# VectorE's decay passes in a fixed order, piece by piece, with the constant tables behind the first piece

## The chip, the cores and the metric

One core of a Trainium2 chip runs the whole program. The metric is the device time of one execution in microseconds; several executions are timed and their median is given. One execution is also profiled. Engines are named as in the profile: PE (TensorE matmul), PEld (TensorE weight load), DVE (VectorE), ACT (ScalarE), POOL (GpSimd) and SP (SyncE, which here only issues transfers).

## The reference

Three layers follow each other. The first is causal attention with a learned decay, for 4 batches of 8 heads, 576 positions, head size 64:

```
s_pos = np.maximum(s, 0.0)
cum = np.cumsum(s_pos, axis=-1)
bias = -(cum[:, :, :, None] - cum[:, :, None, :])
scores = np.where(causal, -1000000000.0, scores + np.minimum(bias, 0.0))
```

followed by a softmax over the row and the product with `v`. The second is a gated layer, `(x @ w1) * (x @ w2) @ w3 @ w_out`, over 2304 tokens, and the third a soft mixture of 8 experts with 4 slots each. The change concerns `cum` alone, the running sum of the positive part of `s` for each of the 32 heads.

## The kernel before

**The decay rows.** `cum` of all 32 heads is made once, at the start, on 32 partitions (one head each). The scores of a head are one matmul over 68 rows: 64 rows of q or k, and 4 rows that hold `cum` in a high and a low part, with their negatives and with ones, so that the product adds `cum_k - cum_q` to the score. `decay_fetch` loads `s` into `dec`. `decay_rows` then works on DVE, with one pass on ACT for each piece:

- `steps(c0, c1)`: L150 takes the positive part times 8, L153 the running sum (the scan of the second stretch starts from the last column of the first).
- for each piece (columns 0 to 320, 320 to 512, 512 to 576): L169 rounds the sum to the matmul's type (high part), L170 subtracts that from the sum (low part), L171 on ACT negates the high part, L172 negates the low part.

`steps` runs twice, for columns 0 to 320 and 320 to 576. The tiles `rows_0` (high) and `rows_1` (low) hold columns up to 512, `rows_2` both parts of the rest. POOL fills the ones of these tiles at L163.

**Who reads them.** The first attention items need query tiles 0 to 2 alone, so columns 0 to 320. Items 0 and 1 (`n < NDIR`) take their rows straight from `rows_0` and `rows_1` by two transfers each (L322, high part first). All later items take them from the DRAM copy `rows_d`, which `decay_store` writes (L176 twice, L177) and L324 reads back.

**What sets the order.** SP's instructions run in program order: `s`, the first word block, q/k of item 0, the second word block, q/k of item 1, the four L322, q/k of item 2 (L300), a word block (L188), L176 twice, L177, q/k of item 3, L324 of item 2, and so on. The order on DVE, ACT, POOL and PE is written by a planner before the run: it lays the program out against its own timeline and places an instruction when what it needs is ready there, so an engine can take later work while an earlier chain waits. A dependency marked `NoSync` between two instructions of one engine fixes their order and adds no semaphore.

**The constant tables.** `masks` builds `rep`, `sel4` and `half` (L789, L791, L794), and `choice_rows`, written at the very end of the program, builds `part` (L962, L965). They need only `ident`, and the planner has put them among the decay passes. `rep`, `sel4`, `half` and `part` are read much later.

**The rest of the start.** Weights come as 64-bit words: `load_words` turns a block into floats with L202 (ACT), L205, L206, L209 (DVE), L233 (ACT) and L234 (POOL). The scores are L359 (PE), the row minimum L362 (DVE), the exponential L367 (ACT), the normalisation L376 and L377 (DVE) and L380 (POOL), the transposes L395 and L409 (PE).

Of the kernel before, what the change touches and what calls it, by code (L numbers as in the profile page):

```python
# [11 lines left out]
F32R = mybir.dt.float32r  # L12
# [4 lines left out]
ALU = mybir.AluOpType  # L17
AX = mybir.AxisListType
# [10 lines left out]
NS = NE * SPE  # L29
# [18 lines left out]
def attn_glu_softmoe_kernel(  # L48
# [14 lines left out]
    nc = tc.nc  # L63
# [55 lines left out]
    ident = cp.tile([P, P], F32, name="ident")  # L119
# [24 lines left out]
    def decay_rows():  # L144
        t0 = dec[0]
        ones = t0[:, 1]
        nc.gpsimd.memset(ones, 1.0)

        def steps(c0, c1):
            nc.vector.tensor_scalar(  # L150
                out=t0[:, 0, c0:c1], in0=t0[:, 0, c0:c1], scalar1=0.0, scalar2=8.0, op0=ALU.max, op1=ALU.mult
            )
            nc.vector.tensor_tensor_scan(  # L153
                out=t0[:, 2, c0:c1], data0=ones[:, c0:c1], data1=t0[:, 0, c0:c1],
                initial=t0[:, 2, c0 - 1 : c0] if c0 else 0.0, op0=ALU.mult, op1=ALU.add,
            )

        rows = [wp.tile([NH, 2, 2, 512], F32, tag="W", name=f"rows_{a}", bufs=NW) for a in range(2)]
        rest = gq.tile([NH, 2, 2, 2, S - 512], F32, tag="g4", name="rows_2", bufs=NG4)
        dec[:] = rows + [rest]  # L160
        for x in rows + [rest]:
            for n in range(2):
                nc.gpsimd.memset(x[:, n, n] if x is not rest else x[:, :, n, n], 1.0)  # L163
        for c0, c1 in ((0, 320), (320, 512), (512, S)):
            if c0 < 512:
                steps(c0, c1 if c1 < 512 else S)
            cum = t0[:, 2, c0:c1]
            p0, p1 = (x[:, :, :, c0:c1] for x in rows) if c1 <= 512 else (rest[:, 0], rest[:, 1])
            nc.vector.tensor_copy(p0[:, 0, 1].bitcast(F32R), cum)  # L169
            nc.vector.tensor_tensor(out=p1[:, 0, 1].bitcast(F32R), in0=cum, in1=p0[:, 0, 1], op=ALU.subtract)  # L170
            nc.scalar.activation(out=p0[:, 1, 0], in_=p0[:, 0, 1], func=AF.Copy, scale=-1.0)  # L171
            nc.vector.tensor_scalar(out=p1[:, 1, 0], in0=p1[:, 0, 1], scalar1=-1.0, scalar2=None, op0=ALU.mult)  # L172

    def decay_store():
        for a in range(2):
# [106 lines left out]
    hd = {}  # L282
# [470 lines left out]
    def run(steps):  # L753
        for _, f in steps:
            f()

    with tc.tile_pool(name="att", bufs=1) as ap:
        phi_sb = ap.tile([P, KC, NS], F32, name="phi_sb")
        u_sb = ap.tile([P, FC, NS], F32, name="u_sb")
        decay_fetch()  # L760
        fetch_words(0, ap)
        att_fetch(0, ap)
        fetch_words(1, ap)
        att_fetch(1, ap)
        make_identity(nc, ident)
        mask = ap.tile([P, S], F32, name="mask")
        nc.gpsimd.memset(mask, 0.0)
        nc.gpsimd.affine_select(
            out=mask[:, S - P :], in_=mask[:, S - P :], pattern=[[-1, P]], base=0,
            channel_multiplier=1, compare_op=ALU.is_ge, fill=NEG,  # L770
        )
        hd["mask"] = mask
        hd["ap"] = ap
        att = att_steps(ap)
        decay_rows()
        for n in range(NDIR):
            att_prep(n, ap)
        att_fetch(2, ap)
        for k in range(2, NRAW):
            fetch_words(k, ap)  # L780
        decay_store()
        for n in range(NDIR, FAR):
            att_fetch(n + 1, ap)
            att_prep(n, ap)

        def masks():

            rep = cp.tile([P, NS], F32, name="rep")
            nc.vector.tensor_reduce(out=rep, in_=ident.rearrange("p (r s) -> p s r", s=NS), axis=AX.X, op=ALU.add)  # L789
            sel4 = cp.tile([P, 4, NS], F32, name="sel4")  # L790
            nc.vector.tensor_copy(sel4, rep.unsqueeze(1).broadcast_to([P, 4, NS]))  # L791

            half = cp.tile([P, 1], F32, name="half")
            nc.vector.tensor_reduce(out=half, in_=ident[:, :64], axis=AX.X, op=ALU.add)  # L794
            return rep, sel4, half

        def load(k):
            i = k // 2 - 1
            if FC <= i < N0:
                (sum_rows if k % 2 else use_rows)(*TODO[i])  # L800
            if k < 2 * N0:
                load_words(k, ap)
            if k + NRAW < 2 * N0:
                fetch_words(k + NRAW, ap)

        def fetch_later(i):
            if i > N0:
                store_words(i - 1)
            if i < len(TODO):
                for e in range(2):  # L810
                    fetch_words(2 * i + e, ap)

        prep = [(1, lambda k=k: load(k)) for k in range(2 * N0 + 2)]
        more = []
        for i in range(N0, len(TODO)):
            more += [(1, lambda i=i: fetch_later(i)), (1, lambda: None)]
            more += [(1, lambda k=2 * i + e: load_words(k, ap)) for e in range(2)] + [(1, lambda: None)]
        more.append((1, lambda: fetch_later(len(TODO))))
        run(weave(att[0], prep[:CA]))
        rep, sel4, half = masks()  # L820
        nc.sync.dma_start(phi_sb, phi)
        steps, late = glu_steps(0, [])
        n1 = int(len(att[1]) * A1)
        run(weave(weave(att[1][:n1], steps[:GB1]), prep[CA:CB1]))
        run(weave(weave(att[1][n1:], steps[GB1:GB]), prep[CB1:CB]))
        k = GC - GB
        steps = steps[GB:]
        run(weave(att[2], weave(steps[:k], prep[CB:]) + steps[k:]))
        for b in range(2, B):
            steps, late = glu_steps(b - 1, late)  # L830
            n = len(more) // (B - b)
            run(weave(weave(att[b + 1], steps), more[:n]))
            more = more[n:]
# [68 lines left out]
    for a in range(0, 4, 2):  # L902
        zt_ps = psum("tp", f"zt_ps_{a}")
        for c in range(2):
            nc.tensor.transpose(zt_ps[:, c * P : (c + 1) * P], z_acc[:, (a + c) * P : (a + c + 1) * P], ident)
        nc.vector.tensor_reduce(
            out=zt[:, a : a + 2], in_=zt_ps[:, : 2 * P].rearrange("p (c t s) -> p c s t", t=2, s=2 * NS),
            axis=AX.X, op=ALU.add,
# [49 lines left out]
    def choice_rows():  # L958
        cb = c_all.rearrange("p (b t) s -> p b t s", t=5)

        for k, m in enumerate((8, 16)):
            nc.vector.tensor_reduce(  # L962
                out=part[:, k, 0:1], in_=ident.rearrange("p (a r s) -> p a r s", r=2, s=m)[:, :, 1], axis=AX.XY, op=ALU.add
            )
        nc.vector.tensor_scalar(  # L965
            out=part[:, :, 1:2], in0=part[:, :, 0:1], scalar1=-2.0, scalar2=1.0, op0=ALU.mult, op1=ALU.add
        )
# [6 lines left out]
        for i4 in range(B):  # L974
# [7 lines left out]
            for blk, (t0, nt, tiles) in enumerate(BLK):  # L982
                tp = psum("sg", f"ctr_ps_{i4}_{blk}")
                for i in tiles:
                    q0, r = QT[i]
# [6 lines left out]
                    out=dst, in0=tp[:, :nt], scalar=part[:, 0, 0:1], in1=dst.bitcast(F32), op0=ALU.mult, op1=ALU.add  # L992
# [34 lines left out]
    order = mybir.DependencyInfo(mybir.DependencyClass.NoSync, mybir.DependencyReason.DATA)  # L1027
# [113 lines left out]
```

## Time and profile before

| | |
|---|---|
| median of 3 runs | 550.87 us (547.64 to 552.92) |
| the profiled execution | 552.43 us |
| its span in the trace | 550.7 us |
| granted TensorE clock, mean | 0.993 |
| busy: PE / DVE / ACT / POOL | 516.8 / 329.0 / 311.6 / 130.6 us |
| instructions | 11764 |

The span is the time from the first to the last instruction of the profiled execution; the 1.7 us between it and that execution's own time lie before and after it. Times in the rows below are microseconds from the start of the span. An engine's busy time leaves out its waits, and PE's ends are modelled.

### The profile page before, as it was taken

Reading aid. Unit: us, or ns where it says so; the run is one execution under the profiler, and the core shown is the slowest. Engines: PE = TensorE matmul, PEld = TensorE weight load, DVE = VectorE, ACT = ScalarE, POOL = GpSimd, SP = SyncE. Lnnn points to the kernel's source line nnn. Section 1 sums busy time; section 2 is a strip of 40 time slices with the busy share of each in tenths; the row PEclk is TensorE's granted clock in tenths of the full one; section 3 lists DMA queues with packets and bytes.
Section 4 is the critical chain, followed back from the end, with each engine's and each line's share of the span. In section 5 each row is a group of like instructions: output and inputs, shape, how many; then the busy total and the mean of one; then the engine's idle time right before and its main releaser. Section 6 shows DMA issues by size and latency. Waiting matters only on the chain.

```text
span 550.7 us, 11764 instructions
## 1 busy us (share of the span) xinstructions
PE 516.8 (94%) x4288; PEld 434.3 (79%) x4288; DVE 329.0 (60%) x1016; ACT 311.6 (57%) x845; POOL 130.6 (24%) x199
## 2 busy tenths in 40 slices
PE   2799899998999999999999999999999999989993
PEld 2567678877788898999989889899989999843452
DVE  7558787879987394866577668566630311252433
ACT  4567667687986674866577567558644211321222
POOL 4475563102454232110221311111310000000000
PEclk9999989999999999999999999999999999999998
DMA  5746973977673253563656537553514999689977
GB/s 147 235 146 193 280 223 128 292 259 269 218 253 102 73 161 113 169 201 133 194 170 211 173 99 208 176 172 114 167 44 137 413 411 376 241 293 423 420 295 241
DMA packets 38809, 118.03 MB, mean 214 GB/s; under 512 B 4224, under 2 KB 10560, under 8 KB 35296
## 3 DMA queue, kind: packets, MB, share of 16 engines
q1 hardware_dynamic: 36768, 113.60, 61.0%
q10 hardware_dynamic: 1984, 3.69, 2.4%
q8 instruction: 34, 0.56, 0.4%
q14 instruction: 23, 0.19, 0.1%
HBM read 102.11 MB, written 11.60 MB: 206 GB/s over the span
## 4 chain that ended last, share of the span: by engine, by line
PE 70%; DMA 13%; DVE 8%; ACT 4%; issue 2%; POOL 1%; SPq 0%; ACTq 0%; DVEq 0%; POOLq 0%
PE gl L457 31%; PE sc_ps L359 7%; PE x_ps L110 7%; PE pt_ps L395 5%; DMA raw_w<-in_w 5%; PE gn_ps L627 3%; PE o_ps L1042 3%; DMA raw_w3t<-in_w3t 3%; PE h_ps L1004 3%; PE ptd_ps L409 2%; PE z_ps L110 2%; DMA raw_wot<-in_wot 2%; DVE sc L362 1%; PE lg L110 1%; ACT sc L367 1%
## 5 line engine op out<-in xcount | busy, mean ns | idle before, releaser
L457 PE MATMUL gl<-x,w12t 128*128 128x320 f32 (+1 forms) x1536 | 237.7, 304 | 0.1
L457 PEld LDWEIGHTS gl<-x,w12t 128*128 128x128 f32 x1536 | 212.7, 190 | 7.4 <-issue 4.4
L380 POOL TENSOR_SCALAR sc<-sc,rinv 128x64 f32<-128x64 f32 (+4 forms) x160 | 101.1, 650 | 253.0 <-DVE rinv L377 85.7
L367 ACT ACTIVATE sc<-sc,nmax 128x64 f32<-128x64 f32 (+4 forms) x160 | 89.8, 563 | 31.4 <-DVE nmax L362 29.1
L362 DVE CUSTOM_DVE_ANT_0 sc<-sc_ps,mask 128x64 f32<-128x64 f32 (+4 forms) x160 | 65.0, 423 | 31.8 <-PE sc_ps L359 31.0
L397 ACT COPY pt<-pt_ps 128x128 f32<-128x128 f32 (+3 forms) x128 | 53.0, 426 | 34.1 <-PE pt_ps L395 25.1
L395 PE MATMUL pt_ps<-ident,sc 128*128 128x128 f32 x320 | 56.6, 286 | 5.5 <-POOL sc L380 3.2
L395 PEld LDWEIGHTS pt_ps<-ident,sc 128*128 128x128 f32 x320 | 38.4, 144 | 16.9 <-POOL sc L380 7.2
L463 ACT COPY a<-gl 128x256 f32<-128x256 f32 (+1 forms) x64 | 25.4, 398 | 46.0 <-PE gl L457 40.7
L359 PE MATMUL sc_ps<-qa 128*128 128x64 f32 (+1 forms) x144 | 46.4, 334 | 1.3 <-DVE gT L475 0.8
L110 PE MATMUL x_ps<-pt,v 128*64 128x256 f32 (+1 forms) x384 | 47.4, 358 | 0.0
L359 PE MATMUL sc_ps<-raw 68*128 68x288 f32 (+4 forms) x96 | 35.8, 516 | 11.6 <-DMA raw<-rows 9.8
L359 PE MATMUL sc_ps<-qb 68*128 68x64 f32 (+1 forms) x144 | 43.6, 306 | 0.9 <-DMA qb<-qa 0.9
L110 PEld LDWEIGHTS x_ps<-pt,v 128*64 128x64 f32 x384 | 33.5, 140 | 5.8 <-issue 1.0
L359 PEld LDWEIGHTS sc_ps<-raw 68*128 68x128 f32 x96 | 21.6, 265 | 16.9 <-issue 14.1
L202 ACT ACTIVATE w_w<-raw_w 128x512 f32<-128x512 f32 x32 | 21.6, 676 | 17.8 <-DMA raw_w<-in_w 17.7
L445 DVE TENSOR_TENSOR x<-x_ps,x 128x320 fp32r<-128x320 f32 (+1 forms) x32 | 14.1, 452 | 29.2 <-ACT x L444 29.2
L630 ACT COPY gn<-gn_ps 128x512 f32<-128x512 f32 x40 | 22.5, 584 | 15.5 <-PE gn_ps L627 15.1
L367 ACT ACTIVATION_READ_ACCUMULATOR sc<-sc,nmax 128x1 f32 x160 | 30.9, 193 | 0.0
L359 PEld LDWEIGHTS sc_ps<-qa 128*128 128x128 f32 x144 | 27.4, 190 | 3.6 <-DVE gT L475 1.3
L409 PE MATMUL ptd_ps<-ident,sc 128*128 128x128 f32 x160 | 25.9, 286 | 3.2 <-ACT pt L397 3.0
L359 PEld LDWEIGHTS sc_ps<-qb 68*128 68x128 f32 x144 | 27.4, 191 | 1.6 <-DVE v_sb L276 1.0
(180 smaller groups left out, 725.6 us busy)
## 6 DMA issues: line engine op xcount, KB each, us to landing
ew<-in_ew SPq DMA_DIRECT2D x27, 1024.0 KB
raw_w<-in_w SPq DMA_DIRECT2D x32, 512.0 KB
raw<-in_qk SPq DMA_DIRECT2D x24, 576.0 KB
v<-in_v SPq DMA_DIRECT2D x16, 576.0 KB
raw_w3t<-in_w3t SPq DMA_DIRECT2D x16, 512.0 KB
raw_wot<-in_wot SPq DMA_DIRECT2D x8, 512.0 KB
raw_wo<-in_wo SPq DMA_DIRECT2D x8, 512.0 KB
w_d<-w_w SPq DMA_DIRECT2D x8, 512.0 KB
```

The source lines that it names most:

```text
L110: mm = nc.tensor.matmul(out_, lhs, rhs, start=start, stop=stop)
L202: line_up(nc.scalar.activation(out=w, in_=hi.bitcast(F32), func=AF.Copy, scale=F64_SCALE))
L359: nc.tensor.matmul(pp[:r, : z - a], x[:, 0, q0 : q0 + r], x[:, 1, a:z], start=x is mul[0], stop=x is mul[-1])
L362: nc.vector.tensor_tensor_reduce(out=sc[:r, a:z], in0=pp[:r, : z - a], in1=hd["mask"][:r, m0 : m0 + z - a], scale=-0.125, scalar=3.0e38 if ...
L367: nc.scalar.activation(out=sc[:r, :W], in_=sc[:r, :W], func=AF.Exp, bias=nmax[:r, i : i + 1], scale=-1.0, accum_out=rsum[:r, i, 0:1],)
L380: nc.gpsimd.tensor_scalar(out=sc, in0=sc, scalar1=rinv[:, i : i + 1], scalar2=1.0, op0=ALU.mult, op1=ALU.mult)
L395: nc.tensor.transpose(tp[:, j * P : (j + 1) * P], sc[:, j * P : (j + 1) * P], ident)
L397: t["turned", i] = nc.scalar.copy(out=pt[:, p0 : p0 + step * (i - 1) + 1 : step], in_=tp[:, : i * P].rearrange("p (j q) -> p j q", q=P))
L409: nc.tensor.transpose(dg[:, p0 : p0 + P], t["sc"][:, c0 : c0 + P], ident)
L457: nc.tensor.matmul(acc[:, :nt], w12_t[fc][:, wi, n, kc], x_t[b, blk, kc][:, xi], start=k == 0, stop=k == 3 * KC - 1)
L463: st["a_copy"] = nc.scalar.copy(out=a_sb[:, :nt], in_=acc[:, :nt])
L630: st["turned", blk, k, h] = nc.scalar.copy(out=gn[:r, 4 * h : 4 * h + 4].rearrange("p c f -> p (c f)"), in_=tp[:r])
```

## The change

Every DVE pass of `decay_rows` is now passed through `line`, which makes it follow the previous one on DVE: L150, L153, L169, L170, L172 of columns 0 to 320, then L150 and L153 of columns 320 to 576, then L169, L170, L172 of columns 320 to 512, and the same three of 512 to 576. The last DVE pass of the first piece is kept as `hd["first"]`, and `after_first` makes four reductions for the tables (`rep`, `half` and the two of `part`) follow it; `sel4` and L965 follow these by their data. Line numbers of before. ACT's passes, the memsets, the transfers and the word conversions have no new dependency.

```diff
+        order = mybir.DependencyInfo(mybir.DependencyClass.NoSync, mybir.DependencyReason.DATA)
+        seq = []
+
+        def line(step):
+            for p in seq:
+                tc.add_manual_dep(step.ins, p.ins.name, order, reason="order")
+            seq[:] = [step]
+
         def steps(c0, c1):
-            nc.vector.tensor_scalar(
+            line(nc.vector.tensor_scalar(
                 out=t0[:, 0, c0:c1], in0=t0[:, 0, c0:c1], scalar1=0.0, scalar2=8.0, op0=ALU.max, op1=ALU.mult
-            )
-            nc.vector.tensor_tensor_scan(
+            ))
+            line(nc.vector.tensor_tensor_scan(
                 out=t0[:, 2, c0:c1], data0=ones[:, c0:c1], data1=t0[:, 0, c0:c1],
                 initial=t0[:, 2, c0 - 1 : c0] if c0 else 0.0, op0=ALU.mult, op1=ALU.add,
-            )
+            ))
...
-            nc.vector.tensor_copy(p0[:, 0, 1].bitcast(F32R), cum)
-            nc.vector.tensor_tensor(out=p1[:, 0, 1].bitcast(F32R), in0=cum, in1=p0[:, 0, 1], op=ALU.subtract)
+            line(nc.vector.tensor_copy(p0[:, 0, 1].bitcast(F32R), cum))
+            line(nc.vector.tensor_tensor(out=p1[:, 0, 1].bitcast(F32R), in0=cum, in1=p0[:, 0, 1], op=ALU.subtract))
             nc.scalar.activation(out=p0[:, 1, 0], in_=p0[:, 0, 1], func=AF.Copy, scale=-1.0)
-            nc.vector.tensor_scalar(out=p1[:, 1, 0], in0=p1[:, 0, 1], scalar1=-1.0, scalar2=None, op0=ALU.mult)
+            line(nc.vector.tensor_scalar(out=p1[:, 1, 0], in0=p1[:, 0, 1], scalar1=-1.0, scalar2=None, op0=ALU.mult))
+            if not c0:
+                hd["first"] = seq[0]
+
+    def after_first(step):
+        order = mybir.DependencyInfo(mybir.DependencyClass.NoSync, mybir.DependencyReason.DATA)
+        tc.add_manual_dep(step.ins, hd["first"].ins.name, order, reason="order")
...
-            nc.vector.tensor_reduce(out=rep, in_=ident.rearrange("p (r s) -> p s r", s=NS), axis=AX.X, op=ALU.add)
+            after_first(nc.vector.tensor_reduce(out=rep, in_=ident.rearrange("p (r s) -> p s r", s=NS), axis=AX.X, op=ALU.add))
...
-            nc.vector.tensor_reduce(out=half, in_=ident[:, :64], axis=AX.X, op=ALU.add)
+            after_first(nc.vector.tensor_reduce(out=half, in_=ident[:, :64], axis=AX.X, op=ALU.add))
...
-            nc.vector.tensor_reduce(
+            after_first(nc.vector.tensor_reduce(
                 out=part[:, k, 0:1], in_=ident.rearrange("p (a r s) -> p a r s", r=2, s=m)[:, :, 1], axis=AX.XY, op=ALU.add
-            )
+            ))
```

## Rows read from the trace of the kernel before

**Rows 1.** Windows view: busy us (instructions) of each engine, clock, DMA share, GB/s.

```profile
2.60:12.00 9.40, 2.21 (x6) 1.91 (x7) 8.93 (x29) 3.72 (x10) 3.85 (x8) 1.00 0.49 154
...
200.00:300.00 100.00, 99.66 (x855) 92.65 (x855) 67.66 (x219) 66.05 (x189) 24.23 (x45) 1.00 0.53 166
```

**Rows 2.** Chain that ended last, 0 to 60: start, us, what.

```profile
11.76 4.84 DMA rows_d<-rows
...
16.66 2.85 DMA raw<-rows_d
...
23.51 6.11 DMA raw_w<-in_w
```

**Rows 3.** Timeline of DVE: start, us, instruction, [idle before, releaser].

```profile
2.67 1.44 DVE L150 TENSOR_SCALAR dec<-dec 32x320 f32<-32x320 f32 x2 [1.81 <-DMA dec<-in_s]
4.04 0.35 DVE L789 TENSOR_REDUCE rep<-ident 128x32 f32<-128x128 f32 x1
4.32 0.80 DVE L153 TENSOR_TENSOR_SCAN dec<-dec 32x320 f32<-32x320 f32 x1
...
5.55 0.31 DVE L169 CAST rows<-dec 32x320 fp32r<-32x320 f32 x1
...
6.49 0.47 DVE L170 TENSOR_TENSOR rows<-dec,rows 32x320 fp32r<-32x320 f32 x1
...
7.50 0.31 DVE L172 TENSOR_SCALAR rows<-rows 32x320 f32<-32x320 f32 x1
...
10.61 0.23 DVE L362 CUSTOM_DVE_ANT_0 sc<-sc_ps,mask 128x64 f32<-128x64 f32 x1
```

**Rows 4.** Timeline of ACT at the start.

```profile
4.75 0.66 ACT L202 ACTIVATE w_w<-raw_w 128x512 f32<-128x512 f32 x1 [2.52 <-DMA raw_w<-in_w]
5.89 0.47 ACT L171 ACTIVATE rows<-rows 32x320 f32<-32x320 f32 x1 [0.48 <-DVE rows L169]
```

**Rows 5.** Timeline of SP's transfer issues, whole and in narrow windows.

```profile
6.45 3.39 SPq L322 DMA_DIRECT2D raw<-rows  x4
...
11.30 0.83 SPq L176 DMA_DIRECT2D rows_d<-rows  x2
```

**Rows 6.** Timeline of SP: the first L322, then the second and third.

```profile
6.45 0.82 SPq L322 DMA_DIRECT2D raw<-rows  x1
...
7.88 1.30 SPq L322 DMA_DIRECT2D raw<-rows  x2
```

**Rows 7.** Timeline of PE: its first matmuls and two later idle times.

```profile
9.79 4.61 PE L359 MATMUL sc_ps<-raw 68*128 68x64 f32 x12 [9.79 <-DMA raw<-rows]
...
19.65 0.66 PE L359 MATMUL sc_ps<-raw 68*128 68x64 f32 x2 [0.95 <-DMA raw<-rows_d]
...
31.93 0.37 PE L110 MATMUL x_ps<-ptd,v 128*64 128x64 f32 x1 [0.85 <-ACT ptd L411]
```

**Rows 8.** DVE groups by form, 2 to 12: busy us, mean ns.

```profile
L150 DVE TENSOR_SCALAR dec<-dec 32x320 f32<-32x320 f32 x1 | 0.8, 835 | 1.8 <-DMA dec<-in_s 1.8
```

**Rows 9.** Timeline of DVE at 30: a step and the one that needs it.

```profile
30.40 0.43 DVE L205 TENSOR_SCALAR w_w<-w_w 128x512 int32<-128x512 int32 x1 [1.87 <-ACT w_w L202]
30.86 0.69 DVE L206 SCALAR_TENSOR_TENSOR w_w<-raw_w,w_w 128x512 int32<-128x512 int32 x1
```

**Rows 10.** Timeline of POOL at the start.

```profile
2.35 2.52 POOL L163 MEMSET rows<- 32x512 f32 x6
4.84 0.37 POOL L768 TENSOR_SCALAR_AFFINE_SELECT mask<-mask 128x128 f32<-128x128 f32 x1
```

**Rows 11.** PE's transposes by line, 38 to 44 and 60 to 70: ns min/median/max.

```profile
L395 PE MATMUL pt_ps<-ident,sc x4: 421/448/476, 39.8 to 43.9; 128*128 128x128 f32 x4
...
L395 PE MATMUL pt_ps<-ident,sc x11: 272/273/329, 60.2 to 66.9; 128*128 128x128 f32 x11
```

**Rows 12.** Windows view of two stretches, columns as in Rows 1.

```profile
34.00:46.00 12.00, 11.80 (x51) 8.95 (x50) 6.38 (x25) 8.00 (x27) 7.89 (x12) 1.00 0.59 173
46.00:68.00 22.00, 19.21 (x135) 15.18 (x134) 18.69 (x45) 16.14 (x42) 12.43 (x11) 1.00 0.89 254
```

## Prediction

> **What bounds the kernel now.** The windows view first: from 200 to 300 us PE is busy 99.66 of 100 us [rows 1]. So in the middle only PE's work counts, and a change in the first microseconds is worth what it brings PE's later work forward, no more. The same view from 2.6 to 12 us shows the other picture: PE is busy 2.21 of 9.4 us and DVE 8.93 [rows 1]. At the start DVE is the full engine. PE's first matmul stands at 9.79, after 9.79 us of idle time that a transfer of the decay rows ended [rows 7].
>
> The chain of waits tells which later events hang on the start: the store of the rows to DRAM from 11.76 to 16.60, the load back from 16.66 to 19.51, and then a word block from 23.51 to 29.62 [rows 2]. PE waits 0.95 us for that load at 19.65 and 0.85 us behind ACT at 31.93 [rows 7]. So the chain runs through SP's queue: store, load, word fetch, each behind the other in program order. SP's issues up to the store have no slack that the trace shows: the four L322 run from 6.45 to 9.84, and the first L176 follows at 11.30 [rows 5] behind one q/k issue and one word issue.
>
> **The change part by part.** *The first piece on DVE.* L150 of 320 columns starts at 2.67, and L172 of the same columns ends at 7.50 + 0.31 = 7.81 [rows 3]. Between them lie the other L150, `rep` (0.35), the other tables in the 0.43 us from the scan's end (4.32 + 0.80 = 5.12) to the cast's start at 5.55, the second scan and its neighbours ahead of L170, and the smaller casts and a word step ahead of L172 [rows 3]. The change removes all of these from the path, apart from a word step that the planner may still put into a gap. What is left is 0.835 [rows 8] + 0.80 + 0.31 + 0.47 + 0.31 [rows 3] = 2.73 us. A step that needs the one just before it starts 0.03 us after its end (30.83 to 30.86) [rows 9], so four such seams add 0.12. The piece ends at 2.67 + 2.85 = 5.52 and its cast at 4.68, where now it is 7.81 and 5.86: 2.29 and 1.18 earlier.
>
> *ACT's pass.* L171 needs the cast, but ACT also has L202 of the first word block, from 4.75 (its transfer) to 5.41, and before the change that goes first [rows 4]. If it stays first, L171 runs from 5.41 to 5.88, and not from 5.89 to 6.36: 0.48 earlier. If the planner turns the two round, L171 runs from 4.71 to 5.18, 1.18 earlier. The cast's end (4.68) and the word's arrival (4.75) lie 0.07 apart, so neither is excluded. I take the order that the row shows, and keep the other as the upper end of the gain.
>
> *SP's queue.* The first L322 comes 0.09 us behind L171's end (6.36 to 6.45) and lasts 0.82; the second waits for L172 (7.81) and goes at 7.88 [rows 6]. After the change L172 is done at 5.52, so that wait is gone and the second L322 follows the first directly, some 0.04 later. With L171 done at 5.88 the first goes at 5.97, the second at 6.83, 1.05 us earlier; with ACT turned round at 5.27 and 6.13, 1.75 earlier. The rest of the queue moves with it: the end of the fourth from 9.84 to 8.79, L176 from 11.30 to 10.25 [rows 5]. PE's first matmul came 1.91 us behind the second issue [rows 7], so it can start at 8.74.
>
> *What is late next.* The scores of items 0 and 1 gain little from that. L362 of the first scores starts at 10.61 with no idle time shown before it [rows 3]: DVE has been busy without a break since 2.67, and the change takes none of that work away. It only moves the tables and the second and third piece behind the first, so for these two items I count nothing. The gain that remains is that of the store: if L176 goes 1.05 us earlier, the rows of item 2 arrive at 18.46 and not at 19.51, and PE, which waited 0.95 us for them [rows 7], waits no longer. The word fetch behind it moves as far. I take 0.95, since PE can't gain more there than it waits.
>
> *The moved work.* The second and third piece are needed at L176, at 10.25. If DVE ran only them after 5.52, they would be done by then: L150 and L153 run once for both, over fewer columns than before, so the five passes of the second piece cost under 2.85 us and the three of the third under 0.31 + 0.47 + 0.31 = 1.09, which ends before 9.46. With the tables and the word steps between them they may end up to about 10.6, where DVE's unbroken stretch ends now [rows 3]; so SP might wait some 0.35 us, and q/k of item 3 and L324 with it, which would leave 0.70 of the gain. The tables themselves cost nothing where they go, as long as their first readers (the logits' sums, the last stage) are tens of microseconds away; without that cover they would cost the 0.71 us that they now take ahead of the cast (0.28 before the scan, 0.43 after it) [rows 3]. The chained passes have up to ten seams; each puts 0.03 us of gap in place of an overlap of up to 0.07 (L150's second end, 4.11, lies behind 4.04 [rows 3]), so 1.0 us at worst is added to DVE ahead of 10.61. No wait on another engine is added, since the edges fix an order on DVE alone.
>
> *POOL beside the first piece.* L150 of 320 columns took 835 ns [rows 8] beside POOL's memsets, which last from 2.35 to 4.87, with L768 behind them to 5.21 [rows 10]; L172, the same form with POOL idle, took 310 [rows 3]. After the change the cast and L172 fall into that time. The row's own bound is a stretch of 835 - 310 = 525 ns for each, so the cast ends between 4.68 and 5.21 and the piece between 5.52 and 6.57: still before L202's end at 5.41 and the second L322 at 6.83, so it takes nothing from the 0.95. It does take from the upper end, where ACT would go round L202: there the gain falls from 1.75 to 1.22. The Trainium skill says in "SBUF — State Buffer", "Who interferes with whom", that a VectorE copy or tensor_scalar in a two-port mode and a GpSimd instruction lock each other out for a whole instruction, whichever starts first. By that rule the cast could stand behind one POOL instruction, and the gain would lean to the lower order; the pair 835 and 310 agrees with it, but no row here separates lock from slowdown.
>
> *The sum.* The profiled execution took 552.43 us, its span 550.7. Less 0.95 that is 551.5. It lies 1.56 above the median of the runs, so against the median of 550.87 the forecast is **549.9**.
>
> **The rivals.** *DVE is the bound.* Its work before 10.61 is the same, so everything up to there stays, the seams add up to 1.0, and the pieces reach L176 late. Then the result is 550.9 to 551.9. For it: DVE's 8.93 of 9.4 us. Against it: the chain goes through the store, not through L362.
>
> *The order is written anew elsewhere (the change does more or less than it says).* The planner gets other ready times in the first 10 us, and its choices on all engines but SP may come out otherwise far behind. What one such choice can cost or bring is one trip of a word block, 6.11 us [rows 2]: 556.0 or 543.8 at the ends, and most such changes smaller.
>
> *PE keeps its long level longer.* Transposes take 421 to 476 ns up to 44 us and 272 to 329 from 60 on [rows 11], with a granted clock of 1.00 in both [rows 12], the 2.4 GHz level, so the grant does not explain it. PE idled for 0.85 us before 31.93 [rows 7] and was busy 11.80 of 12 us from 34 to 46 [rows 12]. If a new order puts an idle time of that size into 34 to 46, the long level may stay to 68: PE's 19.21 busy us there [rows 12] would be 421 / 272 times as long, 10.5 us more, of which its 2.79 idle us take up a part. That gives 549.9 + 7.7 = 557.6, slower. It decides from a gap of about 0.85 us. Against it: the change brings work forward there and opens no gap that I can name.
>
> *PE leaves it sooner.* If the gap at 31.93 closes, since its word block comes earlier, the short level may begin near 34, and 11.80 us shrink by 4.2 to give 545.7.
>
> The Trainium skill ("TensorE: Matmul & The Clock Gate", Part 1) says that the engine's clock is halved by default and that activity releases it; the durations fit that, the granted clock's column does not show it.
>
> **How the numbers follow.** The forecast has 0.52, DVE as the bound 0.18, a new order 0.09 for the better and 0.07 for the worse, the long level kept 0.07, left sooner 0.07. About 1% (5.5 us) is what a measurement of this kernel can tell from no change. Faster by that means under 545.4: half of the better orders, some of the sooner level and a little spread, 0.11. Slower means over 556.4: the long level and the worst orders, 0.09. The rest, 0.80, is the same. The forecast's own range is the runs' spread moved by 0.95, 546.7 to 552.0; with the rivals the range is 545.0 to 555.5.
>
> **What would show it.** The first L172 of 320 columns should end between 5.5 and 6.6, the tables stand behind it, the second L322 go near 6.8 with no wait for DVE, and L176 near 10.3. PE's first matmul should stand near 8.7, the first L362 still near 10.6, and PE's wait of 0.95 before item 2's scores be gone. If L171 stands ahead of L202, the queue moves by 1.2 to 1.75. The forecast is wrong if L176 waits for the last pieces, if the 0.95 comes back as another wait before 60 us, or if the order of PE or ACT beyond 20 us differs from before and the transposes change level at another time than between 44 and 50.

## The result and the profile after

The changed kernel takes 558.99 us (median of 6 runs, 555.27 to 560.79) against 550.29 (6 runs): 1.015 times as long, 95% interval 1.0118 to 1.0182. The forecast was 549.9 with a range up to 555.5, so it was wrong, and on the slower side. The profiled execution of after is the shortest of its runs, 555.27 us with a span of 553.5 and a mean granted clock of 0.979. Ratios here and below leave out executions over 1.5% above the shortest of their kernel, which are two of the four of e6 and one of the ten of e9.

The first piece does what the prediction said, and a little more. Timeline of DVE after the change, which answers to [rows 3]:

```profile
2.63 0.88 DVE L158 TENSOR_SCALAR dec<-dec 32x320 f32<-32x320 f32 x1 [1.77 <-DMA dec<-in_s]
3.61 0.81 DVE L161 TENSOR_TENSOR_SCAN dec<-dec 32x320 f32<-32x320 f32 x1
4.46 0.31 DVE L177 CAST rows<-dec 32x320 fp32r<-32x320 f32 x1
...
5.32 0.31 DVE L180 TENSOR_SCALAR rows<-rows 32x320 f32<-32x320 f32 x1
...
11.45 1.04 DVE L180 TENSOR_SCALAR rows<-rows 32x192 f32<-32x192 f32 x1
...
14.43 0.17 DVE L180 TENSOR_SCALAR rows<-rows 32x64 f32<-32x64 f32 x1
```

The first piece ends at 5.63 instead of 7.81. But the second ends at 12.49 and the third at 14.60, between minima of the scores and word steps, where before the change all three were done by 9.08. ACT's timeline (to [rows 4]) shows the pass ahead of the word block now, the planner having turned the two round:

```profile
4.81 0.47 ACT L179 ACTIVATE rows<-rows 32x320 f32<-32x320 f32 x1 [2.58 <-DVE rows L177]
5.18 0.66 ACT L216 ACTIVATE w_w<-raw_w 128x512 f32<-128x512 f32 x1
```

SP's issues (to [rows 5, 6]), in narrow windows so that single transfers are seen:

```profile
5.37 2.88 SPq L336 DMA_DIRECT2D raw<-rows  x4
...
9.72 0.36 SPq L190 DMA_DIRECT2D rows_d<-rows  x1
...
12.52 0.31 SPq L190 DMA_DIRECT2D rows_d<-rows  x1
14.76 0.66 SPq L191 DMA_DIRECT2D rows_d<-rows  x1
...
16.23 0.72 SPq L338 DMA_DIRECT2D raw<-rows_d  x1
```

The store starts at 9.72, 1.58 earlier than 11.30, and then stands still twice: its second half goes 0.03 behind the end of the second piece (12.49), its last part 0.16 behind the third (14.60). So of the 1.58 us, 0.43 arrive at the load of item 2 (16.23; 16.66 in [rows 2]). PE's timeline (to [rows 7], then on to 54 us):

```profile
8.45 4.61 PE L373 MATMUL sc_ps<-raw 68*128 68x64 f32 x12 [8.45 <-DMA raw<-rows]
...
18.80 2.48 PE L373 MATMUL sc_ps<-raw 68*128 68x64 f32 x6 [0.33 <-DMA raw<-rows_d]
...
40.53 3.75 PE L373 MATMUL sc_ps<-raw 68*128 68x448 f32 x6 [0.82 <-DMA raw<-rows_d]
...
48.08 0.90 PE L423 MATMUL ptd_ps<-ident,sc 128*128 128x128 f32 x3 [0.85 <-ACT pt L411]
...
53.64 2.21 PE L471 MATMUL gl<-x,w12t 128*128 128x320 f32 x6
```

At item 2's scores (18.80) PE is 0.85 ahead of before. That this is close to the forecast 0.95 is luck: 0.43 of it is the earlier issue, and the rest is a load that took 2.43 us (16.23 to 18.66) and not 2.85; in a second trace of the same program (e4 below) these scores start at 19.84, later than before's 19.65. Then, between 38 and 56 us, it falls behind. The same stretch of the kernel before, which [rows 7] did not show:

```profile
40.96 0.48 PE L110 MATMUL x_ps<-ptd,v 128*64 128x64 f32 x2
...
44.37 2.10 PE L359 MATMUL sc_ps<-raw 68*128 68x448 f32 x6
...
47.52 1.96 PE L359 MATMUL sc_ps<-raw 68*128 68x448 f32 x6 [0.61 <-DVE w_w L205]
...
49.78 1.12 PE L457 MATMUL gl<-x,w12t 128*128 128x320 f32 x6
```

Two things differ. The order: item 8's scores (the first group with 448 columns) come behind the values product of items 2 and 3 (`x_ps`, 40.96) before, and ahead of it after, where PE waits 0.82 us for their rows. And the speed: those six matmuls take 3.75 us after and 2.10 before, the first six of the gated layer (`gl`) 2.21 and 1.12. By then PE is 3.86 us late (49.78 to 53.64). The windows view of after shows why they are slow; columns as in [rows 1], the granted clock is the third number from the end:

```profile
38.00:44.00 6.00, 4.89 (x12) 3.00 (x12) 3.59 (x16) 3.84 (x14) 1.78 (x6) 0.53 0.68 181
44.00:50.00 6.00, 4.83 (x31) 3.09 (x30) 3.94 (x10) 3.80 (x11) 4.98 (x6) 0.50 0.36 81
50.00:58.00 8.00, 8.00 (x30) 5.94 (x31) 2.38 (x9) 2.87 (x7) 1.85 (x3) 0.50 0.60 170
58.00:66.00 8.00, 7.93 (x63) 6.18 (x59) 4.33 (x10) 3.75 (x10) 2.50 (x2) 0.94 0.75 224
```

From 38.4 to 58.9 us the clock is at its lower level (0.50, 1.2 GHz). A first rise to full clock (1.00, 2.4 GHz), from 35.0 us, ended at 38.4. One thing about this column had misled the prediction: the trace records the clock only from the first change on, and the view shows 1.00 for the time before the first record. In the kernel before, the first record of full clock starts at 44.8 us, so the 1.00 of [rows 12] before that is no grant, and the transposes of [rows 11] at 448 ns, the scores at 3.75 us for six and the `gl` at 2.21 are the lower level. Item 8's six scores serve as a gauge below: near 1.9 us at full clock, 3.62 or more at half.

### The profile page after: what moved, and what is told of

Same layout as the page of the kernel before. It is cut to its first block, busy times and chain, and to the rows that moved or that the text cites. A ratio compares the mean times of both kernels' runs of the same rounds, so it can differ in the third digit from the quotient of the medians.

```text
span 553.5 us, 11765 instructions
## 1 busy us (share of the span) xinstructions
PE 520.3 (94%) x4288; PEld 433.6 (78%) x4288; DVE 329.6 (60%) x1016; ACT 312.1 (56%) x845; POOL 131.2 (24%) x199
## 4 chain that ended last, share of the span: by engine, by line
PE 72%; DMA 13%; DVE 6%; ACT 4%; issue 2%; SPq 1%; ACTq 0%; DVEq 0%
PE gl L471 32%; PE sc_ps L373 7%; PE x_ps L110 7%; PE pt_ps L409 5%; DMA raw_w<-in_w 5%; DMA raw_w3t<-in_w3t 5%; PE gn_ps L641 3%; PE o_ps L1056 3%; PE h_ps L1018 3%; PE ptd_ps L423 3%; PE z_ps L110 2%; DMA raw_wot<-in_wot 2%; DVE w_w L223 1%; PE lg L110 1%; DVE w_w L220 1%
## 5 line engine op out<-in xcount | busy, mean ns | idle before, releaser
L376 DVE CUSTOM_DVE_ANT_0 sc<-sc_ps,mask 128x64 f32<-128x64 f32 (+4 forms) x160 | 65.4, 423 | 35.8 <-PE sc_ps L373 32.5
L373 PE MATMUL sc_ps<-raw 68*128 68x288 f32 (+4 forms) x96 | 38.0, 540 | 10.4 <-DMA raw<-rows 8.4
L373 PE MATMUL sc_ps<-qb 68*128 68x64 f32 (+1 forms) x144 | 43.6, 306 | 0.0
L248 POOL TENSOR_TENSOR w12t<-w_w,w12t 128x512 fp32r<-128x512 f32 x16 | 23.9, 1496 | 19.7 <-ACT w12t L247 19.7
L489 DVE TENSOR_TENSOR gU<-gl,a 128x256 f32<-128x256 f32 (+1 forms) x20 | 8.7, 435 | 32.8 <-PE gl L471 25.9
```

The costliest lines, as they stand in the source:

```text
L248: nc.gpsimd.tensor_tensor(out=tl, in0=w, in1=th.bitcast(F32), op=ALU.subtract)
L373: nc.tensor.matmul(pp[:r, : z - a], x[:, 0, q0 : q0 + r], x[:, 1, a:z], start=x is mul[0], stop=x is mul[-1])
L376: nc.vector.tensor_tensor_reduce(out=sc[:r, a:z], in0=pp[:r, : z - a], in1=hd["mask"][:r, m0 : m0 + z - a], scale=-0.125, scalar=3.0e38 if ...
```

## The experiments

Most of them change the order in which the engines take their work and nothing else. The order of the planner's finished program of one kernel is given to the other as edges without semaphores, engine by engine; SP's order is the same in all of them.

```diff
+def pin(tc):
+    order = mybir.DependencyInfo(mybir.DependencyClass.NoSync, mybir.DependencyReason.DATA)
+    for text in PINNED.values():          # "PE": "171 175 185 ...", "DVE": ...
+        names = [f"I-{n}" for n in text.split() if int(n) > 83]
+        for a, b in zip(names, names[1:]):
+            tc.add_manual_dep(tc.nc.get_inst_by_name(b), a, order, reason="order")
```

The results together. "Full clock from" is the start of the first record of full clock that lasts over 11 us in the profiled execution, called full clock for good below (falls of 3.4 to 6.8 us later in the span are left aside); the ratio is to the kernel before on the same chip. Five chips were used from e1 on, and before's own median on them lies between 549.90 and 552.26, so ratios compare better than medians do.

| kernel | full clock from, us | median, us | ratio, 95% interval |
|---|---|---|---|
| before | 44.8 | 550.29 | 1 |
| after | 58.9 | 558.99 | 1.015 [1.0118, 1.0182] |
| e1_first_alone | 43.1 | 549.42 | 0.995 [0.9919, 0.998] |
| e2_start_of_after | 58.7 | 558.81 | 1.0108 [1.0049, 1.0168] |
| e3_pe_of_after | 59.9 | 560.46 | 1.0127 [1.0077, 1.0176] |
| e4_after_again | 60.1 | 559.42 (one run) | |
| e5_start_only | 46.2 | 551.08 | 1.0008 [0.9982, 1.0034] |
| e7_before_fill | 44.0 | 554.32 | 1.0059 [1.0027, 1.0092] |
| e8_gap_42 | 54.7 | 555.67 | 1.0072 [1.0036, 1.0108] |
| e9_gap_50 | 43.6 | 553.0 | 1.0019 [0.9988, 1.0051] |
| e10_line_only | 59.0 | 559.34 | 1.015 [1.0096, 1.0204] |
| e11_tables_only | 58.5 | 557.89 | 1.0112 [1.0039, 1.0186] |
| e12_early_before | 43.4 | 550.71 | 1.0001 [0.9977, 1.0026] |
| e13_early_after | 60.1 | 559.18 | 1.0138 [1.0106, 1.0169] |
| e14_first_again | 43.6 | 550.81 | 1.0 [0.9976, 1.0025] |
| e15_item8_back | 61.0 | 560.77 | 1.0217 [1.0176, 1.0259] |
| e16_item8_early | 57.3 | 557.72 | 1.0141 [1.0102, 1.0181] |

**The start alone, and the order alone.** The theory at this point: the start gains, and the loss comes from the planner's order of the later work, which differs from before in 1996 of 3440 places of PE. The rival: the start itself costs, as the pieces come late.

e1: the kernel before in its own order, but for the five passes of the first piece at the front of DVE and L171 ahead of L202 on ACT.

```diff
-    "DVE": "84 137 143 625 138 629 ...",   "ACT": "85 205 141 147 ..."
+    "DVE": "84 137 138 139 140 142 143 ...", "ACT": "85 141 205 147 ..."
```

> The first piece is moved to the front of DVE (five passes in a row) and its pass on ACT ahead of the first word's L202; every other instruction of DVE, ACT, POOL and PE stands in the order of the kernel before, written down by hand. Theory A (the planner's new order of the later work costs the time): PE's first scores near 8.4 as after the change, no loss behind it, 548.8 to 550.3, so 0 to 1.5 under before. Theory B (the lined-up start itself costs, by its seams and by POOL beside it): 553 or more. Theory C (PE's rate, whatever the order): any of the two, with the time following the moment at which the granted clock goes to 1.00 for good.

e2: the kernel after with PE in the order of before, the other engines placed anew by the planner. e3: the kernel before with PE in the order of after.

```diff
+PINNED = {"PE": <PE's order in the other kernel>}
```

> The changed kernel, with PE's order written down as it was before the change; DVE's start is that of the change. Theory A: the 8.7 us come back, 549 to 551. Theory B: it stays at 556 to 560, since the start is that of the change. Theory C: it follows the clock's rise.

> The kernel before, with PE's order written down as it is after the change; DVE's start is that of before, tables among the decay passes. Theory A: slower with nothing of the change in it, 557 to 560. Theory B: 550 to 551, as before. Theory C: it follows the clock's rise.

> The changed kernel once more, for a second trace. Theory A: the same order, 555 to 560, and the loss again between 38 and 55 us where PE's order first departs. Theory C: if this trace shows the granted clock rise at another moment than the first trace (35.0, then half from 38.4 to 58.9), the time moves with it by some 0.4 us for each us of half clock; if the clock differs and the time does not, C falls.

e3 has nothing of the change in its start and takes 560.46; e2 has PE's old order and takes 558.81, not the 549 to 551 of theory A, as the planner places the other engines in another way again (PE waits 1.15 us before 42.91 in it). So the late pieces are not needed for the loss, and PE's order alone is enough but not needed either. e4 loses as after does, and its full clock is as late, but its waits lie elsewhere; PE's timeline:

```profile
32.25 0.45 PE L409 MATMUL pt_ps<-ident,sc 128*128 128x128 f32 x1 [1.15 <-ACT pt L411]
...
42.72 3.75 PE L373 MATMUL sc_ps<-raw 68*128 68x448 f32 x6
...
51.12 0.90 PE L423 MATMUL ptd_ps<-ident,sc 128*128 128x128 f32 x3 [1.69 <-ACT pt L411]
```

From 32.3 to 49.4 us PE is busy 17.09 of 17.10 us there, with item 8's scores at half clock in between. So the wait of 0.82 us before 40.53 in the first trace is not needed for a late rise. e1 stayed at before's level or a little below it. There the store is not held up; in the profile all its operations have one line, L58:

```profile
9.71 1.81 SPq L58 DMA_DIRECT2D rows_d<-rows  x3
...
15.14 0.72 SPq L58 DMA_DIRECT2D raw<-rows_d  x1
```

e5 isolates the start: DVE's first 36 and ACT's first 13 operations in the order of after, everything later in the order of before.

> The changed kernel with all orders written down: DVE's first 36 and ACT's first 13 instructions in the order of the changed kernel (the lined-up pieces, the third one late), everything behind them, and all of PE and POOL, in the order of the kernel before. Theory A (the new order of the later work costs the time): 549 to 552, since the later order is the old one. Theory B (the lined-up start costs, through its late third piece): 556 to 560, and the last store of the rows near 14.8 again.

The ratio is 1.0008: neither loss nor gain.

**Fillers.** If the clock is what costs, extra matmuls might hold it. 28 matmuls of 256 columns without use were put among the early scores and transposes, in after (e6) and in before (e7), with the other order kept.

```diff
+            if n < FILL and i == tiles[0] and m == 0:
+                nc.tensor.matmul(pp[:, :256], ident, hd["mask"][:, S - 256 :], start=True, stop=True)
```

> The changed kernel in its own order, written down, with 28 extra matmuls of 256 columns (results overwritten, no other work) ahead of the scores and the transposes of the first 14 items, so that PE is busy in its early waits. Theory C (PE's long matmul durations up to 59 us are the loss): granted clock at 1.00 for good before 45 us, 549 to 553 in spite of some 10 us of extra PE work. Theory A without the clock (PE starved by the order): no faster than 558, rather 560 to 568 with the extra work.

> The kernel before in its own order, written down, with the same 28 extra matmuls. Theory C: the clock rises earlier than 44.8, and the time comes out within 2 us of the changed kernel with them, 546 to 552. Theory A without the clock: the extra work costs 0 to 10 us, 550 to 560, and the changed kernel with it stays some 8 us above.

e6's four executions took 555.8 to 566.9 us (median 563.82), and the two in its ratio (1.0141, 1.0061 to 1.0221) average 558.9. That is 4.6 us above e7, where after is 8.7 above before; two executions do not tell whether the fillers mended a part of it. They did not bring full clock for good any earlier in e7 (44.0), though they brought a stretch of it, from 26.9 to 37.2, which ended behind a wait of PE of 1.76 us before 35.66. So this pair does not test the clock.

**A wait of its own, ahead of the rise and behind it.** Before's order on all engines, with two passes of POOL over the values, which change nothing in them: of items 2 and 3 (e8), so that PE waits near 41 us, or of items 4 and 5 (e9), so that it waits near 51.

```diff
     def att_pv(n, blk):
+        if n == 2:                       # e9: n == 4
+            vt = hd[n]["v"][:, :5]
+            for _ in range(2):
+                nc.gpsimd.tensor_scalar(out=vt, in0=vt, scalar1=1.0, scalar2=1.0, op0=ALU.mult, op1=ALU.mult)
```

> The kernel before in its own order, written down, with two POOL passes over the values of items 2 and 3 (times 1, nothing changed), put behind the normalisation of item 6, so that PE must wait some 2 us at 41 us, in the stretch ahead of the clock's rise at 44.8. Theory C' (the idle time ahead of the rise puts the rise off, and the long matmul durations up to some 59 us are most of the loss): the clock's rise moves from 44.8 to 48 or later, and the time rises by 5 to 9 us, to 556 to 561. Theory A' (the order costs by waits of its own, not by the clock): the 2 us of wait at most, 550 to 554.

> The control of the run before: the same two passes over the values of items 4 and 5, put behind POOL's step at 48.0, so that PE must wait some 1.5 to 2 us at 51 us, behind the clock's rise. Theory C': 0 to 3 us slower, 551 to 554, unless the clock falls again there. Theory A': the same 0 to 3 us, so that both gaps cost alike.

PE's timeline of e8:

```profile
41.78 0.48 PE L126 MATMUL x_ps<-ptd,v 128*64 128x64 f32 x2 [1.52 <-POOL v L434]
...
45.19 3.62 PE L375 MATMUL sc_ps<-raw 68*128 68x448 f32 x6
...
49.46 3.62 PE L375 MATMUL sc_ps<-raw 68*128 68x448 f32 x6
```

and of e9:

```profile
40.08 0.48 PE L126 MATMUL x_ps<-ptd,v 128*64 128x64 f32 x2
...
43.49 1.95 PE L375 MATMUL sc_ps<-raw 68*128 68x448 f32 x6
46.62 1.96 PE L375 MATMUL sc_ps<-raw 68*128 68x448 f32 x6 [0.73 <-DMA raw<-rows_d]
...
50.64 0.33 PE L126 MATMUL x_ps<-ptd,v 128*64 128x64 f32 x2 [0.64 <-POOL v L434]
```

In e8 PE waits 1.52 us before 41.78 and starts 1.70 us later than in e9, yet the median is 5.05 us over before's (555.67 - 550.62, on this chip). Items 8 and 9 run at half clock, and full clock begins at 54.7. The time lies just under the 556 to 561 that theory C' gave. In e9 the wait falls behind the rise, and the median is 2.4 us over before's, with an interval that holds 1. The waits differ in length (1.52 and 0.64) and the medians by 2.7 us, so the medians alone do not tell the two apart cleanly. PE's busy time on the profile's page does. Of e8:

```profile
PE 521.4 (94%) x4288; PEld 437.1 (79%) x4288; DVE 328.4 (59%) x1016; ACT 311.6 (56%) x845; POOL 131.1 (24%) x201
```

For the same 4288 PE instructions, in the same order, before has 516.8 us and e9 517.0. So PE is busy 4.6 us longer in e8 than in before, and the span is 4.7 us longer (555.4 against 550.7): almost all of this loss is slower matmuls, and not waiting.

**Each part of the change by itself.** e10 leaves out `after_first`, e11 leaves out the line.

```diff
     def after_first(step):               # e10
-        tc.add_manual_dep(step.ins, hd["first"].ins.name, order, reason="order")
+        pass
     def line(step):                      # e11
-                tc.add_manual_dep(step.ins, p.ins.name, order, reason="order")
+                pass
```

> The change without its second half: the decay passes lined up, the tables free, the planner's own order (PE's order differs from before in 37 places of 3440, and not in 1996 as after the change). Theory A: close to before, 548 to 553, as the later order is nearly that of before. Theory B (the late third piece): 556 or more.

> The other half alone: the tables behind the last pass of the first piece, no line through the decay passes, the planner's own order (PE's differs from before in 68 places). Theory A: close to before, 548 to 553. Theory B: close to before as well, since the pieces are not lined up. If one of the halves gives 556 to 560 by itself, a small change of the later order is enough for the whole loss.

Each alone loses about as much as both, and both missed the 548 to 553 of theory A. Theory B had the time of e10, but not for its reason, as e5 has the late third piece and loses nothing. Their programs differ from before in 37 and 68 places of PE, not in 1996. In e10 PE waits ahead of its transposes, in e11 for item 8's rows, and item 8 runs at half clock in both:

```profile
37.66 0.90 PE L423 MATMUL ptd_ps<-ident,sc 128*128 128x128 f32 x3 [0.78 <-ACT pt L411]
...
41.80 3.62 PE L373 MATMUL sc_ps<-raw 68*128 68x448 f32 x6
```

```profile
41.07 3.75 PE L373 MATMUL sc_ps<-raw 68*128 68x448 f32 x6 [1.68 <-DMA raw<-rows_d]
```

**The first 50 us or the rest.** e12 is after with its own start and its own order of all later work, but with what ran in the first 50 us of before in the order of before. e13 is the reverse: the first 50 us as in after, all later work as in before.

```diff
-        PINNED = after's order
+        PINNED = after's first 36 of DVE and 13 of ACT, then before's order to 50 us, then after's   # e12
+        PINNED = after's order to 50 us, then before's                                              # e13
```

> The changed kernel with its own start (first 36 operations of VectorE, first 13 of ScalarE) and its own order of all work behind the first 50 us; what ran in the first 50 us of the kernel before (87 instructions of TensorE, 89 of VectorE, 64 of ScalarE, 49 of GpSimd) stands in the order of the kernel before. Theory (the early order makes TensorE wait about 0.8 us near 40 and 48 us, and its clock is then granted late): the records of full clock begin at 44 to 47 us, the time is 550 to 553 us. Rival (the loss is in the order of the later work, 1952 of 3440 places of TensorE): 557 to 560 us. The two mixed: 553 to 557.

> The other way round: the first 50 us in the order of the changed kernel, all later work in the order of the kernel before. Theory (the early order and the clock): the records of full clock begin at 57 to 61 us, the time is 556 to 560 us. Rival (the later order): 550 to 553 us.

e12 is level with before (1.0001), though it differs from before in 1952 of 3440 places of PE, and from after in 44; e13 loses 1.4%, though it keeps before's order in all but 42. The whole loss is in the first 50 us. PE's rows of e12 and then of e13:

```profile
43.74 1.89 PE L389 MATMUL sc_ps<-raw 68*128 68x448 f32 x6
...
46.92 1.96 PE L389 MATMUL sc_ps<-raw 68*128 68x448 f32 x6 [0.86 <-DMA raw<-rows_d]
```

```profile
43.12 3.75 PE L389 MATMUL sc_ps<-raw 68*128 68x448 f32 x6 [2.41 <-DMA raw<-rows_d]
...
52.76 3.24 PE L389 MATMUL sc_ps<-raw 68*128 68x448 f32 x6 [0.91 <-DMA raw<-rows_d]
```

e12 has a wait of 0.86 us too, but behind the rise (43.4), and loses nothing. In e13 the level even falls back: windows of e13, with the granted clock up at 50 to 53 and down again:

```profile
40.00:49.80 9.80, 7.39 (x33) 4.30 (x31) 6.44 (x18) 5.61 (x15) 4.33 (x8) 0.50 0.28 89
50.00:53.00 3.00, 1.66 (x8) 1.06 (x9) 0.49 (x1) 1.68 (x6) 2.37 (x3) 1.00 0.75 203
53.50:60.00 6.50, 6.50 (x25) 4.75 (x25) 3.17 (x9) 1.54 (x4) 0.00 (x0) 0.50 0.63 173
```

**e1 once more.** e14 is the program of e1, with its lines kept apart in the profile.

> The first piece of the decay passes at the front of VectorE, its copy ahead of the first ScalarE pass of the output queue, all else in the order of the kernel before: the program of the first experiment again. 548 to 551 us if its gain is real (0.995 then), 551 to 552 if that was chance; full clock from 42 to 45 us.

The ratio is 1.0 (0.9976 to 1.0025) where e1 gave 0.995. So the gain of e1 was not repeated, and no version here is shown to beat the kernel before, although item 2's load goes at 14.88 in it:

```profile
14.88 0.71 SPq L340 DMA_DIRECT2D raw<-rows_d  x1
```

**Three instructions.** e15 is after with item 8's three scores behind the values product of items 2 and 3 again; e16 is before with these three ahead of it. Nothing else moves on any engine.

```diff
-    "PE": "... 379 380 381 565 575 578 431 393 ... 444 445 448 ..."
+    "PE": "... 379 380 381 431 393 ... 444 565 575 578 445 448 ..."      # e15; in e16 they move behind 379
```

> The changed kernel in its own order on every engine, but for three matmul instructions of TensorE: item 8's scores stand behind the P-times-values product of items 2 and 3 again, as before. If their place carries the loss (TensorE's 0.82 us wait for item 8's rows near 40 us goes with it), full clock begins by 50 us and the time is 550 to 554 us. If other places of the early order do it as well, a wait of 0.3 us or more stays between 33 and 50 us, full clock begins behind 54 us, and the time is 556 to 560 us.

> The kernel before, with nothing of the change, in its own order but for the same three instructions of TensorE: item 8's scores stand ahead of the P-times-values product of items 2 and 3, as in the changed kernel. If this place carries the loss, TensorE waits 0.8 us or more near 41 us for item 8's rows, full clock begins at 54 to 61 us, and the time is 555 to 560 us. If it takes more than this, full clock stays at 43 to 47 us and the time at 550 to 552 us.

PE's rows of e16, then of e15:

```profile
41.39 3.75 PE L375 MATMUL sc_ps<-raw 68*128 68x448 f32 x6 [0.72 <-DMA raw<-rows_d]
...
51.82 1.96 PE L375 MATMUL sc_ps<-raw 68*128 68x448 f32 x6 [1.71 <-DVE nmax L378]
```

```profile
42.49 0.45 PE L425 MATMUL pt_ps<-ident,sc 128*128 128x128 f32 x1 [1.49 <-ACT pt L427]
...
45.54 3.62 PE L389 MATMUL sc_ps<-raw 68*128 68x448 f32 x6
...
51.37 0.90 PE L439 MATMUL ptd_ps<-ident,sc 128*128 128x128 f32 x3 [1.99 <-ACT pt L427]
```

Three instructions moved in before cost 7.8 us (557.72 against 549.9). To move them back in after does not help, since other places of its early order then make PE wait: 1.49 us before 42.49 and 1.99 before 51.37, both for ACT's copies of earlier transposes (L427), which stand behind word conversions there.

## Why the prediction was wrong

**Right: the first piece.** The cast at 4.46 to 4.77 (forecast 4.68), the piece at 5.63 (5.52), ACT turned round (named as the upper end), PE's first matmul at 8.45 (8.74, or 0.70 earlier with ACT turned round), the first L376 at 10.16 (10.6). Item 2's scores gained 0.85 us (0.95), but in that one trace alone and by luck, as said above; a wait of 0.33 us stayed, and in e4 one of 1.00.

**Wrong in size: the second and third piece.** The step took them as done by about 10.6, with at most 0.35 us of wait at the store. They end at 12.49 and 14.60, the store waits 2.44 us between its halves and 1.93 before its last part, and the load of item 2 keeps 0.43 of the 1.58 us. It was wrong to ask only how much work DVE has: the planner put minima and word steps between the lined-up passes as they came ready. (Its bound on the seams counted ten; the 13 passes have 12, which changes nothing here.) e5 and e12 carry the same late pieces and are level with before, so this cost no measurable time.

**Wrong in kind: the sum took the later order as it was.** Its only later term was 0.95 us of a wait that goes away. That the planner writes the order anew had 0.16, and the long level kept had 0.07 as a rival of its own; both happened, the second through the first. So the step that failed is the one that kept everything behind the start as it was. In its place, the planner's new order of the first 50 us cost 1.4% by itself (e13), and with before's order there the loss was gone (e12, 1.0001). The prediction's own signs of being wrong came: the store waits for the last pieces, PE's order differs beyond 20 us, and the level changes at 58.9.

**Near in part by luck: the long level.** That rival's numbers were near: a wait of about 0.85 us between 34 and 46 was named as the point of decision, and 557.6 as its time. Measured were 0.82 before 40.53 and 558.99. That is in part luck: e4 is as slow without such a wait, and the rival took 7.7 us for the slower matmuls, which cost 3.5 and 3.8 us in the two traces of the changed kernel (next paragraph). It also read the 1.00 of [rows 12] as a grant, which it is not. Its chance was too small for the reason that the prediction gave: that the change "opens no gap that I can name". It did not have to be nameable; e10, e11 and e16 lose with 37, 68 and 18 places of PE's order changed. Changes of DVE's and ACT's first operations alone, with all else kept (e1, e5, e14), were free of it.

**The size from rows.** Full clock for good comes 14.1 us later (58.9 against 44.8). But after also has its first rise of 3.4 us, and before falls back for 3.4 us (78.9 to 82.3), so up to 540 us after has 55.5 us at the lower level and before 48.2: 7.3 more. The lower level stretches the six scores from 1.96 to 3.62 us, 1.85 times, so 7.3 us at it do the work of 3.9, and 3.4 us are lost. PE's busy time agrees: 520.3 us in after and 516.8 in before, 3.5 more, in a span that is only 2.8 longer. This trace is after's shortest execution, 3.7 us under its median. e4, at 559.42, is nearer to the median. Its page has:

```profile
PE 520.6 (93%) x4288; PEld 433.7 (78%) x4288; DVE 331.1 (59%) x1016; ACT 312.0 (56%) x845; POOL 130.9 (23%) x199
```

There PE is busy 3.8 us longer than in before, and the span is 6.9 longer (557.6 against 550.7). So in e4 slower matmuls are a little over half of the loss, and PE's idle time is the rest.

**What is shown and what is not.** Shown: the loss is in the order of the first 50 us (e12, e13); moving three matmuls makes one of its size (e16); two POOL passes that make PE wait ahead of the rise, with every order kept, make full clock later by 10 us and the time longer by 4 (ratio) to 5 (medians), almost all of it in slower matmuls (e8). The time from which full clock is kept is not the same in every run of a program: after has 58.9 and a first rise at 35.0, e4, the same program, 60.1 and none. All kernels in the table with full clock at 54.7 or later are longer by 5 us or more, those with it by 46.2 by under 3.1 us. Of the seven traces with the early rise none has a wait of PE over 0.2 us between 36 us and its rise; of the other ten all have one of 0.7 us or more between 37 and 44 us, except e4. Not shown: what sets the late rise in the changed kernel. Its first trace has waits of 0.34, 0.29, 0.82 and 0.85 us between 35 and 49 us; e4 has none between 32.3 and 49.4. In both, item 8's scores stand ahead of the values product. Whether the place of the matmuls acts on the clock without any wait is a rival that no run tests: e16 moves them and gets a wait of 0.72 us with it, and e15 moves them back and gets one of 1.49.

## What to carry to other kernels

An edge that only fixes the order of a few early operations gives a planner other ready times, and what it writes tens of microseconds later may cost many times what the edge gains: keep the old order of the rest in place when a small change is timed, and then see whether the planner's own answer differs. While TensorE is still at its lower clock, look at its waits before anything else: waits of 0.7 to 2.4 us there went with 5 to 11 us here, one of 0.9 us behind the rise with none. One trace of the changed kernel was as slow without such a wait, so a second trace is worth taking before a wait is blamed. Read the level from the duration of one repeated matmul group, and not from a clock column that has no record yet.

## What the runs showed of the hardware

**A long stretch at the lower level.** Full clock for good came at 43 to 61 us of the span, with single rises of 3.4 to 10.2 us ahead of it in some traces. In after PE was busy 12.83 of 14.00 us from 41 to 55 us at a granted 0.50. The Trainium skill says in "TensorE: Matmul & The Clock Gate", Part 1, that the engine is throttled by default and that activity releases it; the runs agree with the default, and in after the release for good came only at 58.9.

**DVE beside POOL.** The prediction allowed the cast and L172 a stretch of 525 ns each, from the 835 ns of [rows 8]. Neither was stretched: beside the memsets the cast took 314 ns (306 before), and L172's successor L180 took 314 (308). But the second piece's L180 took four times as long beside POOL's L248 (10.98 to 12.38) as L172 had in before (241 ns), where POOL was idle; DVE groups by form, after:

```profile
L180 DVE TENSOR_SCALAR rows<-rows 32x192 f32<-32x192 f32 x1 | 1.0, 1037 | 0.0
...
L177 DVE CAST rows<-dec 32x320 fp32r<-32x320 f32 x1 | 0.3, 314 | 0.0
```

The Trainium skill ("SBUF — State Buffer", "Who interferes with whom") lets a VectorE tensor_scalar or cast in a two-port mode and a GpSimd instruction each block the other for a whole instruction, whichever starts first. L180 ends 0.11 us behind L248, which agrees; the cast, beside memsets of 558 ns each, shows no such wait; whether either of them ran in a two-port mode the trace does not tell.
